# First loads of an attention and token-MLP kernel: weight quarters from two DMA queues put on one, in another order and split

## The chip, the cores and the metric

The kernel runs on one core of a Trainium2 chip. The metric is the device time of one execution in microseconds. The median of three runs before the change is 168.17 us (168.17, 168.17 and 168.28). All times below count from the start of the profiled span, in us.

## What is computed

The input is a sequence of 2048 rows of 512 (S = 2048, D = 512), all in bfloat16. Two mixers see the same rows and are blended by a gate per row:

```
qkv = x @ wqkv                       # 32 heads of 16
logits[s, w] = q[s] . k[s - 2w] / 4  # w = 0..7, only rows that exist
a = softmax(logits) @ v[s - 2w] @ wo

h = layernorm(x)                     # over the 512 columns
u = gelu(h^T @ w1 + b1)              # token MLP, 2048 -> 1792
b = (u @ w2 + b2)^T                  # 1792 -> 2048

g = sigmoid(sum(x * gate_w))
out = g * a + (1 - g) * b
```

x is A_x throughout; the layer norm, the projections and the gate all read it.

## The kernel before

**The work and its stages.** One program of about 2150 instructions. TensorE runs, in this order: a warm-up, the q and k projections of the first 512 rows, the other q and k projections, the v projections (all L619), the row sums of the q times k products (L698, in two bursts of 64), the first MLP product (L812), the second (L862) and the output projection (L878). VectorE computes the layer norm statistics (L574), the products of q and shifted k (L690), the gate sums (L674), parts of the softmax, the products with v and their sums (L797, L800, L802) and the last combination (L899). ScalarE copies results out of PSUM (L627 for q, L630 for k and v, L728 for logits, L833 gelu, L930) and normalizes rows (L598). GpSimd builds an identity matrix and zeroes paddings.

**The order.** Every operation is added to a list scheduler (`_Sched`) with a duration, the buffers it reads and writes (`reads`, `writes`), operations that it waits for (`deps`) and operations that it only follows on the same engine (`after`, `order`). The scheduler orders each engine's instructions by planned times, and semaphore waits are worked out from `deps`. A DMA given a `lands` has that planned landing time; it is used for the order alone. `chain` (L943) fixes the order on VectorE, on ScalarE and on parts of the DMA queue by hand. `last_main` chains the large matmuls in the order in which they are written.

**The first loads.** The transposed rows XT have four column blocks of 128 (block 0 to 3). For the first 512 rows:

- `d_xp` (L479, SyncE) loads the plain columns 0 to 127 of the 512 rows, 128 KB. TensorE transposes them with the identity (`f_tr`, L545, four matmuls in two operations); ScalarE copies one half (L555) and VectorE the other (L557) into column block 0 of XT.
- `d_xt0` (L473, SyncE) is a transposing DMA of the columns 128 to 511, which fills blocks 1 to 3.
- Wq, Wk and Wv are column thirds of `wqkv`; a "quarter" is the 128 rows of one that belong to one column block. `ld_w(tn, d0, n)` (L447) loads n quarters of third tn from block d0 on. The first two quarters of Wq are issued by ScalarE, two more by SyncE, then Wk in two loads of two quarters.
- After them SyncE issues `d_x0` (rows 0 to 255 for the layer norm), `d_xt1` (the transposing DMA of the next 512 rows, `ld_xt`, L460), `d_x2`, `d_x4`, `d_xt2`, `d_xt3`, `d_x8`, `d_x12`, Wv, W1 and the rest.

`throttle()` makes most later loads wait for the landing of the fifth-last one in the list `init_dmas`; `first_loads` have their waits cleared (L489).

**The first projections.** Eight PSUM banks hold q (banks 0 to 3) and k (4 to 7) of the first 512 rows, each a sum over four column blocks. L635 writes the order: q with block 0, q with 1, q with 2, q with 3, k with 0 and 1, k with 2 and 3. These are 32 matmuls; then follow the groups of four of `seq_proj` (L645) for other rows, in banks 0 to 3 again. Before them `f_warm` (L533) runs matmuls on constants: six of 512 columns (`warm1`), one of 256 (`warm2`), then the transposes, then one of 512 (`warm3`).

Of the kernel before, what the change touches and what calls it, by code (L numbers as in the profile page):

```python
# [13 lines left out]
D = 512  # L14
# [319 lines left out]
def bass_gated_mix__sliding_local_dilated__mixer_token_mlp__prompt_kernel(nc, A_x, A_wqkv, A_wo, B_x, B_w1, B_b1, B_w2, B_b2, gate_w, out, dbg=None):  # L334
    with contextlib.ExitStack() as es:
# [79 lines left out]
        A = sch.add  # L415
# [31 lines left out]
        def ld_w(tn, d0, n, q="sp"):  # L447
            ds = sch.dsem("wqkv%d_%d" % (tn, d0))
            op = sch.dma(q, mk_dma(WQKV[:, d0:d0 + n, tn * D:(tn + 1) * D], wqkv_v[:, d0:d0 + n, tn * D:(tn + 1) * D]),
                         n * 128 * D * 2, ds, writes=["wqkv%d_%d" % (tn, dt) for dt in range(d0, d0 + n)],  # L450
                         deps=throttle() if q == "sp" and n == 4 else [], after=prev_dma() if q == "sp" else [],
                         issue=0.65 if n == 4 else 0.45, name="d_wp%d_%d" % (tn, d0))
            if q == "sp":
                init_dmas.append(op)
            return op
# [14 lines left out]
        def ld_xt0():  # L470
            ds = sch.dsem("xt0")
            dst = XT[:, 1:4, 0:512]
            op = sch.dma("sp", lambda e: e.dma_start_transpose(dst, x2d[0:512, 128:512]), 512 * 384 * 2, ds, issue=1.25,  # L473
                         writes=XT0[1:4], after=prev_dma(), name="d_xt0")
            init_dmas.append(op)
            return op

        XP = view("OUTS", BF16, [(128, 4), (1, 128)])
        d_xp = sch.dma("sp", mk_dma(XP, xv[:, 0:4, 0:128]), 512 * 128 * 2, sch.dsem("xp"), writes=["outs0"], issue=0.4, name="d_xp")  # L479
        d_xp.lands = 3.9  # L480
        init_dmas.append(d_xp)

        first_loads = [ld_w(0, 0, 1, "act"), ld_xt0(), ld_w(0, 1, 1, "act"), ld_w(0, 2, 1), ld_w(0, 3, 1), ld_w(1, 0, 2), ld_w(1, 2, 2),
                       ld_x(0, 2)]
        ld_xt(1)
        first_loads.append(init_dmas[-1])
        for op_, t_ in zip(first_loads, (3.5, 5.7, 5.0, 6.3, 6.7, 7.6, 8.6, 9.4, 11.0)):
            op_.lands = t_
            op_.deps.clear()  # L489
        first_loads[2].order.add(first_loads[0])  # L490
        init_dmas[:] = [first_loads[1]] + first_loads[5:]
        ld_x(2, 2)
        ld_x(4, 4)
        ld_xt(2)
# [51 lines left out]
                return ins  # L546
            return fn

        A("pe", f_warm(6), 2.56, writes=["lg7_0", "lg7_1"], name="warm1", prio=-100)
        w2_ = A("pe", f_warm(1, 256), 0.2, writes=["lg7_0", "lg7_1"], name="warm2", prio=-100)  # L550
        ta_ = A("pe", f_tr(0), 0.215, reads=["outs0", "ident"], writes=["lg5_0", "lg5_1"], after=[w2_], name="tr0", prio=-100)
        tr_ = A("pe", f_tr(1), 0.215, reads=["outs0", "ident"], writes=["lg6_0", "lg6_1"], after=[ta_], name="tr1", prio=-100)
        A("pe", f_warm(1), 0.43, writes=["lg7_0", "lg7_1"], after=[tr_], name="warm3", prio=-100)
        w3_ = tr_
        A("act", lambda e: e.activation(out=XT[:, 0, 0:256], in_=ps[:, 5, 0:256], func=AF.Copy), 0.35, reads=["lg5_0", "lg5_1"],  # L555
          writes=["xt0_0"], name="ev_tra", prio=0)
        A("dve", lambda e: e.tensor_copy(out=XT[:, 0, 256:512], in_=ps[:, 6, 0:256]), 0.35, reads=["lg6_0", "lg6_1"],  # L557
# [74 lines left out]
        tnames = ["q", "k", "v"]  # L632
        first = [(tn, dl) for tn in range(2) for dl in range(4)]
        fbn = [["acc%d" % b] for b in range(4)] + [["lg%d_0" % b, "lg%d_1" % b] for b in range(4, 8)]
        for (b0, d0, d1, s0, s1) in ((0, 0, 1, 0, 512), (0, 1, 2, 0, 512), (0, 2, 3, 0, 512), (0, 3, 4, 0, 512), (4, 0, 2, 0, 512), (4, 2, 4, 0, 512)):  # L635
            for b in range(b0, b0 + 4):
                tn, dl = first[b]
                last_main[0] = A("pe", f_proj(tn, dl, 0, b, d0, d1, s0, s1), 0.216 * (d1 - d0) * (s1 - s0) / 512,
                                 reads=xt_of(0, d0, d1) + ["wqkv%d_%d" % (tn, dt) for dt in range(d0, d1)],
                                 writes=fbn[b], after=[last_main[0]], name="pf_%s%d_%d_%d" % (tnames[tn], dl, d0, s0))  # L640
                last_main[0].order.add(w3_)
# [411 lines left out]
```

## Time and profile before

| what | value |
|---|---|
| median of three runs | 168.17 us |
| the profiled execution's own time | 168.55 us |
| its span, first to last instruction | 167.3 us |
| TensorE busy | 163.9 us, 98% |
| VectorE busy | 151.3 us, 90% |
| ScalarE busy | 75.0 us, 45% |
| DMA moved | 29.64 MB, mean 177 GB/s |
| d_xp, issue to landing | 0.80, 3.1 us |
| first Wq quarters on ScalarE, issue to landing | 0.80 and after 1.02 us both issued, 2.9 and 3.0 us |
| d_xt0, issue, length of its issue, to landing | 1.29, 1.64, 4.4 us |
| d_xt1, the same | 5.58, 3.25, 5.5 us |
| first projection matmul | 5.15 |

In timelines each row has the start, the time that it covers, the engine ("SPq" and "ACTq" are the DMA issues of SyncE and ScalarE, "PEld" TensorE's weight loads), the line, the operation, output and input, a count, and in brackets the idle time ahead of it with what ended it. All SBUF tiles are views of one arena, so the line tells more than the name. A matmul's recorded length includes time in which the next one already runs; the distance between starts is its pace. In a table of stretches, each row gives the busy time of each engine in that stretch, then the clock, the share of the DMA engines and what they moved.

### The profile page before, as it was taken

Reading aid. Unit: us, or ns where it says so; the run is one execution under the profiler, and the core shown is the slowest. Engines: PE = TensorE matmul, PEld = TensorE weight load, DVE = VectorE, ACT = ScalarE, POOL = GpSimd, SP = SyncE. Lnnn points to the kernel's source line nnn. Section 1 sums busy time; section 2 is a strip of 40 time slices with the busy share of each in tenths; the row PEclk is TensorE's granted clock in tenths of the full one; section 3 lists DMA queues with packets and bytes.
Section 4 is the critical chain, followed back from the end, with each engine's and each line's share of the span. In section 5 each row is a group of like instructions: output and inputs, shape, how many; then the busy total and the mean of one; then the engine's idle time right before and its main releaser. Section 6 shows DMA issues by size and latency. Waiting matters only on the chain.

```text
span 167.3 us, 2152 instructions
## 1 busy us (share of the span) xinstructions
PE 163.9 (98%) x860; PEld 77.6 (46%) x860; DVE 151.3 (90%) x154; ACT 75.0 (45%) x116; POOL 0.7 (0%) x8
## 2 busy tenths in 40 slices
PE   7999999999999999999999999999999999999994
PEld 2455555554454444444444444444444444444463
DVE  0145999999999999999999999999999999999896
ACT  3077688889899818793113121131231321310100
POOL 1000000000000000000000000000000000000000
DMA  5999999968003837996579936462672580000454
GB/s 130 315 272 262 303 322 291 307 196 246 0 0 97 311 115 187 303 290 153 133 183 343 335 129 143 112 187 68 184 218 83 138 223 0 0 0 0 157 190 159
DMA packets 47625, 29.64 MB, mean 177 GB/s; under 512 B 9856, under 2 KB 46464, under 8 KB 47616
## 3 DMA queue, kind: packets, MB, share of 16 engines
q1 hardware_dynamic: 45504, 24.85, 54.0%
q10 hardware_dynamic: 2112, 4.66, 10.0%
q8 instruction: 7, 0.11, 0.3%
q14 instruction: 2, 0.02, 0.0%
HBM read 21.24 MB, written 2.10 MB: 140 GB/s over the span
## 4 chain that ended last, share of the span: by engine, by line
PE 94%; DVE 3%; DMA 2%; issue 0%
PE ps L812 29%; PE ps L862 29%; PE ps L619 25%; PE ps L878 6%; PE ps L698 4%; DVE arena L899 2%; DMA arena<-in_A_x_dram 2%; PE ps L545 0%; DVE arena L557 0%
## 5 line engine op out<-in xcount | busy, mean ns | idle before, releaser
L812 PE MATMUL ps<-arena 128*128 128x512 bf16 x224 | 48.7, 379 | 0.0
L862 PE MATMUL ps<-arena 128*128 128x512 bf16 x224 | 48.7, 379 | 0.0
L619 PE MATMUL ps<-arena 128*128 128x512 bf16 x192 | 42.3, 382 | 0.1
L690 DVE TENSOR_TENSOR arena<-arena 128x4096 bf16<-128x4096 bf16 (+1 forms) x12 | 35.5, 2996 | 2.3 <-ACT arena L630 1.8
L797 DVE TENSOR_TENSOR arena<-arena 128x8192 bf16<-128x8192 bf16 x8 | 35.0, 4419 | 0.0
L812 PEld LDWEIGHTS ps<-arena 128*128 128x128 bf16 x224 | 21.8, 98 | 26.7 <-ACT arena L728 0.4
L862 PEld LDWEIGHTS ps<-arena 128*128 128x128 bf16 x224 | 21.9, 98 | 26.5
L619 PEld LDWEIGHTS ps<-arena 128*128 128x128 bf16 x192 | 21.6, 114 | 20.8 <-DVE arena L557 0.7
L930 ACT ACTIVATE arena<-ps,arena 128x512 bf16<-128x512 f32 x16 | 12.4, 778 | 39.4 <-PE ps L862 39.4
L800 DVE TENSOR_TENSOR arena<-arena 128x4096 bf16<-128x4096 bf16 (+1 forms) x16 | 27.0, 1752 | 0.0
L630 ACT ACTIVATE arena<-ps 128x512 bf16<-128x512 f32 x32 | 18.5, 596 | 4.5 <-PE ps L619 4.5
L833 ACT ACTIVATE arena<-ps,arena 128x512 bf16<-128x512 f32 x14 | 9.6, 687 | 22.2 <-PE ps L812 17.4
L574 DVE BATCH_NORM_STATS2 arena<-arena 128x6 f32<-128x512 bf16 x16 | 10.0, 680 | 5.6 <-DMA arena<-in_A_x_dram 5.6
L878 PE MATMUL ps<-arena 128*128 128x512 bf16 (+1 forms) x80 | 14.2, 337 | 0.0
L899 DVE SCALAR_TENSOR_TENSOR arena<-ps,arena 128x512 bf16<-128x512 f32 (+1 forms) x20 | 11.5, 638 | 0.9 <-PE ps L878 0.7
L598 ACT ACTIVATE arena<-arena 128x512 bf16<-128x512 bf16 x16 | 12.2, 806 | 0.0
L627 ACT ACTIVATE arena<-ps 128x512 bf16<-128x512 f32 x16 | 9.0, 596 | 5.5 <-PE ps L619 5.4
L878 PEld LDWEIGHTS ps<-arena 128*128 128x128 bf16 x80 | 7.8, 98 | 6.3
L674 DVE SCALAR_TENSOR_TENSOR arena<-arena 128x512 bf16<-128x512 bf16 x16 | 10.1, 685 | 0.0
L744 DVE TENSOR_TENSOR arena<-arena 128x512 bf16<-128x512 bf16 (+4 forms) x11 | 7.3, 667 | 0.6 <-ACT arena L763 0.2
L698 PE MATMUL ps<-arena 128*32 128x512 bf16 x128 | 7.3, 380 | 0.0
L728 ACT ACTIVATE arena<-ps 128x512 bf16<-128x512 f32 x8 | 4.7, 592 | 4.6 <-PE ps L698 4.6
(42 smaller groups left out, 40.5 us busy)
## 6 DMA issues: line engine op xcount, KB each, us to landing
arena<-in_B_w_dram SPq DMA_DIRECT2D x7, 1024.0 KB, 8.3
arena<-in_B_w_dram SPq DMA_DIRECT2D x8, 896.0 KB, 5.1
arena<-arena ACTq DMA_DIRECT2D x32, 128.0 KB, 3.0
arena<-in_A_x_dram SPq DMA_DIRECT2D x4, 512.0 KB, 5.1
out_dram<-arena SPq DMA_DIRECT2D x14, 128.0 KB, 1.7
arena<-in_A_x_dram SPq DMA_DIRECT2D x1, 1536.0 KB, 7.9
arena<-in_A_wqkv_dram SPq DMA_DIRECT2D x2, 256.0 KB, 3.6
arena<-in_A_x_dram SPq DMA_DIRECT2D x2, 256.0 KB, 3.5
```

Of the source, the lines that this page charges most:

```text
L598: A("act", (lambda t_: (lambda e: e.activation(out=X[:, t_, :], in_=X[:, t_, :], func=AF.Identity, scale=col(RSTD, t_), bias=col(NMR, t_)) ...
L619: ins = e.matmul(ps[:, bank, s0:s1], lhsT=lhsT, rhs=XT[:, dt, sb * 512 + s0:sb * 512 + s1], start=(dt == 0 and s0 == 0), stop=(dt == 3))
L630: return lambda e: e.activation(out=dst, in_=ps[:, bank, :], func=AF.Copy)
L690: return lambda e: e.tensor_tensor(out=PBL[buf][:, :, 512 * c0:512 * (c0 + nc_)], in0=in0, in1=in1, op=ALU.mult)
L698: ins = e.matmul(ps[32 * c:32 * c + 32, 4 + wl, :], lhsT=RP, rhs=PBL[buf][:, wl, c * 512:(c + 1) * 512], start=(dl == 0), stop=(dl == 3), ...
L797: A("dve", (lambda o_, i0, i1: (lambda e: e.tensor_tensor(out=o_, in0=i0, in1=i1, op=ALU.mult)))(pv, in0, in1), 4.4, reads=v_res + ["atx_% ...
L800: A("dve", (lambda pv_, n__: (lambda e: e.tensor_tensor(out=pv_[:, 0:n__], in0=pv_[:, 0:n__], in1=pv_[:, n__:2 * n__], op=ALU.add)))(pv, n ...
L812: ins = e.matmul(ps[:, bank, :], lhsT=W1W[:, slot, st, 128 * e_:128 * e_ + 128], rhs=X[:, st, :], start=(st == 0), stop=(st == NST - 1))
L862: ins = e.matmul(ps[:, bank, :], lhsT=W2S[slot][:, ft, 128 * e_:128 * e_ + 128], rhs=UT[:, ft, :], start=(ft == 0), stop=(ft == NFT - 1))
L878: ins = e.matmul(ps[:, bank, 0:c1 - c0], lhsT=OT[:, t, 128 * i:128 * i + 128], rhs=WO[:, t, c0:c1], start=(t == 0), stop=(t == 3))
L899: A("dve", (lambda i_, b_, c0_, c1_: (lambda e: e.scalar_tensor_tensor(out=T1[:, i_, c0_:c1_], in0=ps[:, b_, 0:c1_ - c0_], scalar=col(G, i ...
L930: A("act", (lambda i_, bank_: (lambda e: e.activation(out=T1[:, i_, :], in_=ps[:, bank_, :], func=AF.Identity, scale=col(OMG, i_), bias=co ...
```

## The change

d_xp is issued first, as before. Behind it, on SyncE alone, stand now: the first quarter of Wq, the first of Wk, d_xt0, the second quarter of Wq, the second of Wk, then quarter 3 of both in one DMA and quarter 4 of both in one DMA (`ld_qk`, 256 KB each), d_xt1, d_x0. ScalarE issues none of them. d_xt1 waits until d_xt0 has landed. The first 32 projections take the order q and k with block 0, q and k with block 1, q with 2, q with 3, k with 2 and 3. The warm-up has five instead of six matmuls of 512 columns, one of 256 is added after `warm3`, and the projections follow it. The planned landing times are changed with it.

```diff
         d_xp = sch.dma("sp", mk_dma(XP, xv[:, 0:4, 0:128]), 512 * 128 * 2, sch.dsem("xp"), writes=["outs0"], issue=0.4, name="d_xp")
-        d_xp.lands = 3.9
-        init_dmas.append(d_xp)
-
-        first_loads = [ld_w(0, 0, 1, "act"), ld_xt0(), ld_w(0, 1, 1, "act"), ld_w(0, 2, 1), ld_w(0, 3, 1), ld_w(1, 0, 2), ld_w(1, 2, 2),
-                       ld_x(0, 2)]
+
+        def ld_qk(d):
+            ds = sch.dsem("wqk%d" % d)
+            op = sch.dma("sp", mk_dma(WQKV[:, d, 0:2 * D], wqkv_v[:, d, 0:2 * D]), 2 * 128 * D * 2, ds,
+                         writes=["wqkv0_%d" % d, "wqkv1_%d" % d], after=prev_dma(), issue=0.45, name="d_wqk%d" % d)
+            init_dmas.append(op)
+            return op
+
+        first_loads = [ld_w(0, 0, 1), ld_w(1, 0, 1), ld_xt0(), ld_w(0, 1, 1), ld_w(1, 1, 1), ld_qk(2), ld_qk(3)]
         ld_xt(1)
         first_loads.append(init_dmas[-1])
-        for op_, t_ in zip(first_loads, (3.5, 5.7, 5.0, 6.3, 6.7, 7.6, 8.6, 9.4, 11.0)):
+        first_loads.append(ld_x(0, 2))
+        for op_, t_ in zip(first_loads, (4.0, 4.4, 6.1, 6.5, 6.9, 7.6, 8.3, 11.3, 12.0)):
             op_.lands = t_
             op_.deps.clear()
-        first_loads[2].order.add(first_loads[0])
-        init_dmas[:] = [first_loads[1]] + first_loads[5:]
+        d_xp.lands = 3.1
+        first_loads[7].deps.add(first_loads[2])
+        first_loads[0].order.add(d_xp)
+        init_dmas[:] = [first_loads[2]] + first_loads[5:]
...
-        A("pe", f_warm(6), 2.56, writes=["lg7_0", "lg7_1"], name="warm1", prio=-100)
+        A("pe", f_warm(5), 2.13, writes=["lg7_0", "lg7_1"], name="warm1", prio=-100)
...
         A("pe", f_warm(1), 0.43, writes=["lg7_0", "lg7_1"], after=[tr_], name="warm3", prio=-100)
-        w3_ = tr_
+        w3_ = A("pe", f_warm(1, 256), 0.2, writes=["lg7_0", "lg7_1"], after=[tr_], name="warm4", prio=-100)
...
-        for (b0, d0, d1, s0, s1) in ((0, 0, 1, 0, 512), (0, 1, 2, 0, 512), (0, 2, 3, 0, 512), (0, 3, 4, 0, 512), (4, 0, 2, 0, 512), (4, 2, 4, 0, 512)):
-            for b in range(b0, b0 + 4):
+        for (b0, nb, d0, d1, s0, s1) in ((0, 8, 0, 1, 0, 512), (0, 8, 1, 2, 0, 512), (0, 4, 2, 3, 0, 512), (0, 4, 3, 4, 0, 512),
+                                         (4, 4, 2, 4, 0, 512)):
+            for b in range(b0, b0 + nb):
```

## Prediction

> **What bounds the kernel now.** I read the chain of work that ended last first, in order of time, because it tells which engine an earlier arrival would have to help.
>
> ```profile
> 0.80 3.10 DMA arena<-in_A_x_dram
> ...
> 4.04 0.60 PE ps L545 x4
> ...
> 4.66 0.44 DVE arena L557
> ...
> 5.15 33.44 PE ps L619 x152
> ...
> 161.68 3.98 DVE arena L899 x9
> ```
>
> The first transfer (d_xp) lands at 3.90, TensorE transposes it (L545), VectorE copies it out (L557), and from 5.15 to 161.68 every piece of the chain is TensorE (94% of the span by the page). So whatever lets the first projection matmuls (L619) be further along, and starves nothing later, takes the same time off the end. Those matmuls do not all run at one pace. Next, the timeline of the start (start, length, engine, count), and narrow windows of it for single starts:
>
> ```profile
> 0.84 2.93 PE L537 MATMUL ps<-const-bfloat16-1.0 128*128 128x512 bf16 x7 [0.84 <-PEq L1038]
> ...
> 5.14 0.15 PEld L619 LDWEIGHTS ps<-arena 128*128 128x128 bf16 x2 [0.68 <-DVE arena L557]
> ...
> 5.56 0.15 PEld L619 LDWEIGHTS ps<-arena 128*128 128x128 bf16 x1 [0.27 <-issue]
> ...
> 5.98 10.97 PEld L619 LDWEIGHTS ps<-arena 128*128 128x128 bf16 x51 [0.28 <-issue]
> ```
>
> The matmuls start at 5.15, 5.56, 5.98, 6.26 and 6.48, then every 0.216 us. The warm-up matmuls (L537; weight loads at 1.22, 1.64, 2.07, 2.50, 2.92) came every 0.42 to 0.43, so TensorE runs at half pace until a switch. The one that starts at 5.98 takes 0.28: u/0.427 + (0.28-u)/0.216 = 1 gives u = 0.13, so the switch is at 6.11. It is 5.27 us after the first warm-up matmul (0.84). The stretch table shows a clock of 1.00 throughout, so the pace is all that shows it. **A start that is earlier by x before 6.11 gains only half of x**, if the switch stays.
>
> Last, SyncE's queue, read with the times to landing of single DMA issues:
>
> ```profile
> 1.29 1.64 SPq L473 DMA_TRANSPOSE arena<-in_A_x_dram  x1
> 2.99 2.03 SPq L429 DMA_DIRECT2D arena<-in_A_wqkv_dram  x4
> 5.07 0.47 SPq L429 DMA_DIRECT2D arena<-in_A_x_dram  x1
> 5.58 3.25 SPq L460 DMA_TRANSPOSE arena<-in_A_x_dram  x1
> 8.87 1.09 SPq L429 DMA_DIRECT2D arena<-in_A_x_dram  x2
> ```
>
> With its time to landing, each ends at: d_xt0 1.29+4.4 = 5.7; the two quarters of Wq 2.99+3.1 = 6.1 and 3.59+2.9 = 6.5; Wk 4.08+3.4 = 7.5 and 4.55+3.8 = 8.35; d_x0 9.07; d_xt1 5.58+5.5 = 11.1. With matmul number 3 (counted from 0) at 6.26 and 0.216 each after it, TensorE needs them at number 4 (6.48), 8 (7.34), 12 (8.2), 16 (9.1) and 24 (10.8), and d_xt1 at number 32 (12.5). All are early by 0.8 us or more; only d_xp binds.
>
> **d_xp lands earlier.** Two Wq quarters (128 KB each) leave ScalarE's queue, where they were issued at 0.80 and about 1.3 beside d_xp (128 KB), and stand behind it on SyncE. The stretches about it (busy time by engine, then clock, DMA share and GB/s):
>
> ```profile
> 1.90:2.10 0.20, 0.20 (x2) 0.03 (x1) 0.00 (x0) 0.20 (x1) 0.00 (x0) 1.00 0.25 61
> 2.10:2.30 0.20, 0.20 (x2) 0.12 (x1) 0.00 (x0) 0.20 (x1) 0.00 (x0) 1.00 0.33 84
> 2.30:2.50 0.20, 0.20 (x2) 0.00 (x1) 0.00 (x0) 0.20 (x1) 0.00 (x0) 1.00 0.64 100
> 2.50:2.70 0.20, 0.20 (x2) 0.14 (x1) 0.00 (x0) 0.20 (x1) 0.00 (x0) 1.00 0.67 166
> 2.70:2.90 0.20, 0.20 (x1) 0.00 (x0) 0.00 (x0) 0.20 (x1) 0.00 (x0) 1.00 1.06 339
> ```
>
> The DMA engines are not full until 2.7. The first four sum to 82 KB, about half of it d_xp's. Alone it has some 87 KB left; at the 330 GB/s after 2.7 that is 0.26 us, to 2.96. Transfers here land 0.45 to 0.8 us after the share falls (d_x0 falls about 8.6, lands 9.07; d_xt1 10.3 and 11.1): 3.4 to 3.75. If it had had all the early bytes, 128 KB are reached at 2.85 and it lands from 3.3. The ends are the nearest rows: a 128 KB store takes 1.7 us (lands 2.5), its own row 3.1 (lands 3.9). I take 3.25, nearer the byte count than the store; the planner's due time of 3.1 is only declared.
>
> The Trainium skill, DMA: Bandwidth & Descriptors, section "Issuing engines are not separate DMA queues", says that DMAs of all issuing engines share the same 16 engines and interleave, and that several issuers save only issue time. By it the shift costs issue time and gains only what no longer interleaves with d_xp; the shares under 1 before 2.7 mean that little of that may be there, and then the first rival below holds.
>
> **From landing to the first matmul.** Landing to L545 took 4.04-3.90 = 0.14, L545 to the first projection 1.11 (4.04 to 5.15). One 512-column warm-up less ends that burst at 3.77-0.42 = 3.35, which is before 3.25+0.14 = 3.39, so it does not delay. After the transposes (4 of about 0.11) come 0.43 and the added 256-column one (0.21): 1.07, just inside the copy's 1.11; their cost is 0, and 0.2 if the copy were quicker. The first projection starts at 4.50, earlier by 0.65. By 6.11 it has done 4.50, 4.92, 5.34, 5.77 at half pace; the fourth has 0.34/0.427 = 0.80 behind it and ends at 6.15, where the kernel before reaches that point at 6.48. **Gain 0.33.** At the bounds of the landing: 2.5 is cut off by the warm-up burst (start about 4.46, gain 0.35); 3.9 gives 0.
>
> **Are later operands in time?** New queue, plain issues at 0.51 each including the gap: d_xp 0.80, Wq quarter 1.29, Wk quarter 1.80, d_xt0 2.33 to 3.97, Wq and Wk second quarters 4.03 and 4.6, d_wqk2 5.1, d_wqk3 5.6 to 6.07, then the wait. The bytes are the same 1 MB of Wq and Wk, the count of issues the same 10 (SyncE 8 to 10, ScalarE 2 to 0). A transposing transfer landed 2.2 to 2.8 us after its issue ended (2.93 to 5.7; 8.83 to 11.1): d_xt0 6.15, or 6.73 by its whole 4.4. After it the bytes went at 0.4 us per 128 KB: 6.5, 6.9, 7.7, 8.5; or, by old latencies of 3.0 to 4.0 from issue, 7.1, 7.6, 8.9, 9.6. The needs, 0.33 earlier for each number and in the new order (q and k of block 0, q and k of block 1, then q of 2, q of 3, k of 2 and 3; numbers 8, 12, 16, 20): 7.01, 7.87 for Wk's second quarter, 8.74, 9.60. I take the early ends, since the same bytes move and only the first half us at the start has fewer in flight: cost 0; the late ends cost 0.1 to 0.16. First quarters land by 1.29+3.1 = 4.4 and 4.9, need 4.50 and 6.15.
>
> **The added wait.** SyncE stands at the wait from 6.07 to d_xt0's landing (6.15; 6.73 at worst) and behind it are d_xt1, d_x0, d_x2, d_x4, the two later transposing transfers and all of W1. The 3.25 of d_xt1's issue ends when the bytes ahead have drained (d_x0's at about 8.5); the one with a free line ahead took 2.03 and the 384-column one 1.64, or 2.19 for 512. Now only Wk's 0.5 MB is ahead and d_x0 is behind: 6.2+2.2 = 8.4 to 9.4, landing 10.6 to 11.7; need 12.2. Cost 0; if d_xt0 lands at 6.73 and the old 5.5 counts from there, 12.3, and 0.1 is lost. d_xt3, before 17.8, needs 19.9: a shift of 1 us is covered.
>
> **VectorE.** d_x0 now lands at 11.3 to 12.5 and d_x2 to 13.1; four statistics (1.29 a pair) end by 13.9 to 14.7. The first product (L690) started at 15.08 on ScalarE's copy of block 1; ScalarE now copies q later (bank 0 is done at 9.96, eight copies at 0.49 to 13.95, then block 1), so this copy ends at 15.05 again: VectorE starts as before. Two later rows have the room:
>
> ```profile
> 42.20 4.43 DVE L690 TENSOR_TENSOR arena<-arena 128x8192 bf16<-128x8192 bf16 x1 [0.41 <-PE ps L698]
> 157.36 8.29 DVE L899 SCALAR_TENSOR_TENSOR arena<-ps,arena 128x512 bf16<-128x512 f32 x15 [0.72 <-PE ps L878]
> ```
>
> It waits for TensorE there, 0.41 and 0.72, so it can follow a TensorE earlier by up to 1.1. Cost 0; a VectorE late by over 0.8 would begin to eat the gain.
>
> **Sum.** -0.33 from the start, 0 for the rest. The profiled execution took 168.55 with a span of 167.3 (1.25 around it); it becomes 168.22. It lies 0.38 over the median of 168.17, so the runs should give 167.84: I say **167.85**.
>
> **Rivals.** (1) *Nothing moves.* d_xp is bound by something other than company (shares under 1 in its first 0.8 us) and lands at 3.7 to 3.9, or operands come at their late ends (7.1 for 7.01, 12.3 for 12.2) and take 0.2 back: 168.05 to 168.2. (2) *The switch moves with the work.* If full pace comes after so much busy time, before it had 2.93+0.86+0.96 = 4.75 us by 6.11 with 0.5 us of holes; the new order has 2.51 by 3.35 and almost no hole, and reaches 4.75 at 5.65. By then 2.7 matmuls are done, by 6.11 4.8 against 2.3: gain 0.54; with a switch earlier still, up to 0.84, where the second Wq quarter at 6.5 binds (number 8 was at 7.34): 167.3 to 167.65. For it: the switch fell 5.27 after the first matmul though 4.75 were busy. Against: nothing here shows two switches to compare. (3) *The switch is lost.* One warm-up less leaves TensorE idle from 3.35 to d_xp's landing + 0.14. Before, that hole was 0.27 (3.77 to 4.04). If a longer hole restarts the count, from a landing past 3.48 the switch comes 5.27 after the transposes, at about 8.9 instead of 6.11, and half of 2.8, less the gain of 0.2, is lost: 169.4; a partial restart, 168.5 to 169.4. Against: 0.27 was survived, and the added matmul closes the 0.25 before 5.15.
>
> The Trainium skill, TensorE: Matmul & The Clock Gate, Part 1, has windows of about 3.4 us that run free of the kernel and release the clock after a busy one. By it the switch sits at a boundary whatever the extra work does, as in my sum, which would be 0.33 by it and 0.54 by counted work. Its phase would differ from run to run; the three runs, within 0.11 us, do not show that.
>
> **Chances.** Forecast 0.40 (gain 0.1 to 0.4), rival 1 0.15, rival 2 0.25, rival 3 0.20, with any case of operands so late that they cost over 0.4. About 0.2% (0.34 us) is what a measurement can tell from no change. The forecast splits at it, 0.16 above and 0.24 below: faster 0.16+0.25 = 0.41, same 0.24+0.15 = 0.39, slower 0.20. The range leaves out most of rival 3 and the far end of rival 2: 167.35 to 168.6; the forecast's own is 167.75 to 168.1.
>
> **What would show it.** d_xp landing at 3.1 to 3.4 and L545 0.14 later; the first L619 near 4.5; weight loads 0.42 apart up to the switch, and where it falls (6.1: forecast; 5.7 or less: rival 2; 8 or later: rival 3); no hole in L619 near 7.0, 8.7, 9.6 and 12.2; d_xt1 landed by 11.7; the VectorE wait of 0.41 at 42 shorter or gone. A landing of d_xp as late as 3.9 or a hole over 0.3 in L619 would make it wrong.

## The result and the profile after

The changed kernel takes **168.65 us** in the median of 21 runs (168.20 to 169.42); beside it the kernel before took 168.18 us in 21 runs (167.84 to 168.91). The ratio, worked out from all the runs and so not exactly that of the two medians, is 1.0025, with a 95% interval of 1.0014 to 1.0036: **slower, by 0.47 us between the medians**. 167.85 had been predicted.

The profiled execution of the changed kernel took 168.50 us, with a span of 167.2. Before, these were 168.55 and 167.3. So the two profiled executions are level although the medians are 0.47 us apart. That is the first thing to explain: one of the two is not typical of its kernel. The execution of 168.55 is slower than 17 of the 21 times of the kernel before; that of 168.50 is below the median of its own.

The changed lines move the numbers: L545 becomes L552, L537 L544, L557 L564, L619 L626, L690 L698 and L899 L907. The chain of work that ended last, in order of time (start, length, what):

```profile
3.34 0.55 PE ps L552 x4
...
4.53 2.74 PE ps L626 x8
7.31 6.42 PE ps L626 x29
...
161.65 3.98 DVE arena L907 x9
```

The transposes start at 3.34 instead of 4.04: the first transfer (d_xp) did land earlier. But the last VectorE chain starts at 161.65 instead of 161.68. The break between the eighth projection and the ninth, at 7.31, shows where to look. TensorE's weight loads of the changed kernel:

```profile
4.41 0.14 PEld L626 LDWEIGHTS ps<-arena 128*128 128x128 bf16 x2 [0.57 <-DVE arena L564]
...
6.10 0.15 PEld L626 LDWEIGHTS ps<-arena 128*128 128x128 bf16 x1 [0.28 <-issue]
6.46 0.33 PEld L626 LDWEIGHTS ps<-arena 128*128 128x128 bf16 x2 [0.21 <-issue]
7.28 1.45 PEld L626 LDWEIGHTS ps<-arena 128*128 128x128 bf16 x8 [0.49 <-issue]
```

The projections begin at 4.41, 0.74 us earlier than before (5.15). They run at half pace, one every 0.42, up to a switch at about 6.39 (the step from 6.10 to 6.46 is 0.36, so 0.29 of it is at half pace). After it number 5 starts at 6.46, and number 8 could start at 6.46 + 3 x 0.216 = 7.11. It starts at 7.31, and number 16 at 9.04. Before, number 8 started at 7.34 and number 16 at 9.07. So 0.74 us of earlier start has become 0.03 within eight matmuls: half pace and a switch 0.28 us later take 0.51, and a wait of 0.20 for the second quarter of Wq takes the rest.

SyncE's queue of the changed kernel (start, length of the issues, line, operation, count):

```profile
0.80 0.45 SPq L429 DMA_DIRECT2D arena<-in_A_x_dram  x1
1.31 0.96 SPq L429 DMA_DIRECT2D arena<-in_A_wqkv_dram  x2
2.32 1.86 SPq L473 DMA_TRANSPOSE arena<-in_A_x_dram  x1
4.23 2.00 SPq L429 DMA_DIRECT2D arena<-in_A_wqkv_dram  x4
6.71 2.81 SPq L460 DMA_TRANSPOSE arena<-in_A_x_dram  x1
```

and times to landing, as the list of DMA issues in the first 20 us has them (KB each, median us):

```profile
arena<-in_A_wqkv_dram SPq DMA_DIRECT2D x4, 128.0 KB, 2.9
arena<-in_A_wqkv_dram SPq DMA_DIRECT2D x2, 256.0 KB, 3.7
arena<-in_A_x_dram SPq DMA_DIRECT2D x1, 128.0 KB, 2.4
```

d_xp lands at 0.80 + 2.4 = 3.2. The issue of d_xt0 begins a microsecond later than before (2.32 against 1.29) and lasts 1.86, and in that time SyncE sends nothing else. d_xt0 lands at 6.7. The four loads behind it, each with its own latency, land at 4.23 + 2.95 = 7.2 (Wq's second quarter), 4.86 + 2.8 = 7.7 (Wk's), 5.32 + 3.6 = 8.9 (d_wqk2) and 5.80 + 3.8 = 9.6 (d_wqk3). The wait before d_xt1 is 6.23 to 6.71.

What that queue does to the DMA engines is in the table of stretches (busy time by engine, then clock, DMA share, GB/s). The kernel before:

```profile
3.00:3.90 0.90, 0.77 (x3) 0.07 (x1) 0.00 (x0) 0.13 (x1) 0.00 (x0) 1.00 1.18 317
3.90:4.80 0.90, 0.76 (x5) 0.45 (x5) 0.14 (x1) 0.35 (x1) 0.00 (x0) 1.00 1.28 278
```

and the changed kernel:

```profile
3.00:3.90 0.90, 0.90 (x7) 0.56 (x6) 0.00 (x0) 0.19 (x1) 0.00 (x0) 1.00 0.58 188
3.90:4.80 0.90, 0.90 (x3) 0.14 (x2) 0.42 (x1) 0.20 (x1) 0.00 (x0) 1.00 0.85 115
```

From 1.8 to 4.8 the kernel before moves 722 KB and the changed one 509; by 8.4 it is 1871 against 1469. A second execution of each (b1 and a1 below) has 712 against 516 by 4.8 and 1720 against 1486 by 8.4. The bytes to be moved are the same. They are sent later.

VectorE did not hold TensorE back. At 42.18 its wait for TensorE ahead of the second product (L698) is 0.38 (before 0.41).

### The profile page after: what moved, and what is told of

Same layout as the page of the kernel before. It is cut to its first block, busy times and chain, and to the rows that moved or that the text cites. A ratio compares the mean times of both kernels' runs of the same rounds, so it can differ in the third digit from the quotient of the medians.

```text
span 167.2 us, 2138 instructions
## 1 busy us (share of the span) xinstructions
PE 163.3 (98%) x846; PEld 77.7 (46%) x860; DVE 151.1 (90%) x154; ACT 74.8 (45%) x116; POOL 0.7 (0%) x8
## 3 DMA queue, kind: packets, MB, share of 16 engines
q10 hardware_dynamic: 1824, 4.39, 9.4%
## 4 chain that ended last, share of the span: by engine, by line
PE 96%; DVE 2%; issue 1%
PE ps L870 29%; PE ps L820 29%; PE ps L626 25%; PE ps L886 6%; PE ps L706 4%; DVE arena L907 2%; PE ps L544 2%; PE ps L552 0%
## 5 line engine op out<-in xcount | busy, mean ns | idle before, releaser
L626 PE MATMUL ps<-arena 128*128 128x512 bf16 x188 | 42.5, 385 | 0.4 <-ACT arena L594 0.2
L698 DVE TENSOR_TENSOR arena<-arena 128x4096 bf16<-128x4096 bf16 (+1 forms) x12 | 35.4, 2994 | 0.4 <-PE ps L706 0.4
L626 PEld LDWEIGHTS ps<-arena 128*128 128x128 bf16 x192 | 21.6, 114 | 21.4 <-issue 1.8
L938 ACT ACTIVATE arena<-ps,arena 128x512 bf16<-128x512 f32 x16 | 12.5, 778 | 39.4 <-PE ps L870 39.4
L637 ACT ACTIVATE arena<-ps 128x512 bf16<-128x512 f32 x32 | 18.7, 599 | 3.2 <-PE ps L626 3.1
L634 ACT ACTIVATE arena<-ps 128x512 bf16<-128x512 f32 x16 | 9.3, 603 | 8.1 <-PE ps L626 8.1
L907 DVE SCALAR_TENSOR_TENSOR arena<-ps,arena 128x512 bf16<-128x512 f32 (+1 forms) x20 | 11.5, 638 | 0.9 <-PE ps L886 0.7
L736 ACT ACTIVATE arena<-ps 128x512 bf16<-128x512 f32 x8 | 4.7, 592 | 4.6 <-PE ps L706 4.6
```

The lines of the kernel that those rows point to most:

```text
L626: ins = e.matmul(ps[:, bank, s0:s1], lhsT=lhsT, rhs=XT[:, dt, sb * 512 + s0:sb * 512 + s1], start=(dt == 0 and s0 == 0), stop=(dt == 3))
L637: return lambda e: e.activation(out=dst, in_=ps[:, bank, :], func=AF.Copy)
L698: return lambda e: e.tensor_tensor(out=PBL[buf][:, :, 512 * c0:512 * (c0 + nc_)], in0=in0, in1=in1, op=ALU.mult)
L907: A("dve", (lambda i_, b_, c0_, c1_: (lambda e: e.scalar_tensor_tensor(out=T1[:, i_, c0_:c1_], in0=ps[:, b_, 0:c1_ - c0_], scalar=col(G, i ...
L938: A("act", (lambda i_, bank_: (lambda e: e.activation(out=T1[:, i_, :], in_=ps[:, bank_, :], func=AF.Identity, scale=col(OMG, i_), bias=co ...
```

## The experiments

Each kernel was run beside the kernel before on the same chip; the ratios are to that kernel, with a 95% interval. The theories, by the letters that some expectations use: the single line of SyncE brings the later operands late (A, later L); the switch of pace moves or is lost (S); the shorter warm-up costs (C); the added wait costs (W); the last transposing DMA, d_xt3, comes too late (D).

**e1: the second quarters on ScalarE.** The changed kernel, with both second quarters on ScalarE's queue, in program order behind an added one-element activation that was to keep them clear of d_xp.

```diff
-first_loads = [ld_w(0, 0, 1), ld_w(1, 0, 1), ld_xt0(), ld_w(0, 1, 1), ld_w(1, 1, 1), ld_qk(2), ld_qk(3)]
+first_loads = [ld_w(0, 0, 1), ld_w(1, 0, 1), ld_xt0(), ld_w(0, 1, 1, "act"), ld_w(1, 1, 1, "act"), ld_qk(2), ld_qk(3)]
+tab_ = A("act", lambda e: e.activation(out=col(TH, 0), in_=nc.const_aps.tensor(1.0, [128, 1], BF16), func=AF.Copy), ...
+first_loads[3].order.add(tab_)
+first_loads[4].order.add(first_loads[3])
```

> The changed kernel, but the second quarters of Wq and Wk are issued by ScalarE, behind a one-element copy that has the activation table loaded first (so from about 2.3 us, and not beside d_xp). Theory A (one line runs dry: while SyncE spends 1.86 us issuing d_xt0, nothing else is issued, the DMA engines move 110 to 220 GB/s from 3.0 to 4.8 where they moved 250 to 350, and the operands of matmuls 8 and 16 land at 7.1 and 8.9, which gives the early start back): both quarters land by 6.0, the wait at matmul 8 shrinks to what d_xt0 (6.7) sets, the one at matmul 16 goes because d_wqk2 is issued 1 us earlier; 0.2 to 0.5 us under the changed kernel's 168.65: 168.15 to 168.45. Theory W (the added wait costs it, by d_xt1 and all behind it): d_xt0 lands no earlier, the wait ends no earlier, so 168.5 to 168.8. Theory C (the shorter warm-up makes full pace come later): no change, 168.5 to 168.8.

169.23 (168.05 to 170.61, 12 runs), ratio 1.0058 [1.0026, 1.0089]. The edit did not do what it was meant to. ScalarE in its trace:

```profile
0.86 0.97 ACTq L429 DMA_DIRECT2D arena<-in_A_wqkv_dram  x2
2.09 0.20 ACT L478 ACTIVATE arena<-const-bfloat16-1.0 128x1 f32<-128x1 bf16 x1
```

The loads went out at 0.86, beside d_xp, though they stand behind the activation that ran at 2.09. d_xp landed at 3.9, as before the change, and the start was 5.18. That shows what held d_xp in the kernel before: two loads in its company cost it 0.7 us. The spread of 2.4 us, even without the slowest run, is new; the profiled execution (168.10) is at its lower end and does not show its cause.

**e2: the wait away.**

```diff
-        first_loads[7].deps.add(first_loads[2])
```

> The changed kernel without the wait of d_xt1 for d_xt0. A: d_xt1 is issued at about 6.25 instead of 6.71 and lands earlier, but TensorE did not wait for it, so the same time, 168.5 to 168.8. W: back to 168.2 or under. C: 168.5 to 168.8.

168.79 (168.22 to 169.83, 12), 1.0034 [1.0013, 1.0056]. The loss stays, so the added wait is not its cause.

**e3: the sixth warm-up matmul back.**

```diff
-        A("pe", f_warm(5), 2.13, writes=["lg7_0", "lg7_1"], name="warm1", prio=-100)
+        A("pe", f_warm(6), 2.56, writes=["lg7_0", "lg7_1"], name="warm1", prio=-100)
```

> The changed kernel with six instead of five long warm-up matmuls, so the first projection starts about 0.4 us later, at 4.8. A: the operands of matmuls 8 and 16 are what it waits for (7.1, 8.9), so the later start costs only part of 0.4: 168.65 to 168.85, and the wait at matmul 8 is gone or smaller. C: full pace comes earlier again and 168.2 or under results. If the early start were worth half of itself, as the prediction had it, 168.85 to 168.9.

169.20 (168.52 to 169.72, 11), 1.0044 [1.0023, 1.0064]. The shorter warm-up is not the cause either. Its switch came early, at 5.1, and the ninth matmul then waited 0.36 for the weights. The matmuls of its trace also show a second floor that I had not priced:

```profile
7.17 13.12 PE L626 MATMUL ps<-arena 128*128 128x512 bf16 x59 [0.36 <-DMA arena<-in_A_wqkv_dram]
21.26 9.01 PE L626 MATMUL ps<-arena 128*128 128x512 bf16 x40 [0.96 <-DMA arena<-in_A_x_dram]
```

Number 68 is the first that needs d_xt3, and it stood 0.96 us, until d_xt3 had landed at 21.1.

**e4 and e5: a start that is the same in every execution.** To take the switch out of the comparison, I held back the first projections of the kernel before until d_xt1 (e4) or d_x0 (e5) had landed, and filled the time with warm-up matmuls.

```diff
-        A("pe", f_warm(1), 0.43, writes=["lg7_0", "lg7_1"], after=[tr_], name="warm3", prio=-100)
-        w3_ = tr_
+        w3_ = A("pe", f_warm(21), 5.0, writes=["lg7_0", "lg7_1"], after=[tr_], name="warm3", prio=-100)
-                                 reads=xt_of(0, d0, d1) + ["wqkv%d_%d" % (tn, dt) for dt in range(d0, d1)],
+                                 reads=xt_of(0, d0, d1) + xt_of(1) + ["wqkv%d_%d" % (tn, dt) for dt in range(d0, d1)],
```

e5 has `f_warm(14)` there, and `deps=[first_loads[7]]` on the first projections in place of `xt_of(1)`.

> The kernel before, with 21 long warm-up matmuls behind the transposes and the first projection held until d_xt1 has landed (11.1), so that every execution starts its projections at full pace and at a landing. About 168.18 + 5.6 to 6.0 = 173.8 to 174.2. If the spread of the kernel's runs (167.84 to 168.91 in 21) comes from a switch of pace that falls at another time in each execution, the 5 or more runs of this one lie within 0.4 us; if it comes from elsewhere, they spread over 0.7 us or more.

> The kernel before, with 14 instead of one long warm-up matmuls behind the transposes and the first projection held until d_x0 has landed (9.1 to 9.7), so TensorE idles under 2 us and starts its projections after the switch of pace in every execution. Theory S (the switch falls at another time in each execution; in the traces so far at 6.1, 6.4, under 5.2, under 4.7, about 5.1 and 4.3; half of what lies between 5.15 and it is lost): 172.0 to 172.8 with a spread under 0.7 us, where the kernel before spreads over 1.1 to 1.4. If the spread of the kernel before comes from its transfers or later stages: the same 1.1 to 1.4 or more here.

e4: 176.29 (175.26 to 178.11, 6); e5: 173.69 (172.49 to 174.39, 4). Both failed as a test: the runs spread over 1.3 us (e4, without its slowest) and 1.9 us (e5), where under 0.4 and 0.7 had been expected. The warm-up was too short and TensorE idled ahead of the first projection (3.35 us by its matmuls in e4, 2.15 in e5). e5's weight loads, and the stretches of its trace, show what can follow:

```profile
9.64 0.80 PEld L618 LDWEIGHTS ps<-arena 128*128 128x128 bf16 x5 [2.62 <-issue]
...
13.95 0.98 PEld L618 LDWEIGHTS ps<-arena 128*128 128x128 bf16 x5 [0.21 <-issue]
```

```profile
10.46:13.87 3.41, 3.41 (x10) 1.18 (x8) 1.56 (x3) 0.00 (x0) 0.00 (x0) 0.50 1.05 287
```

After the idle time five loads come at full pace, then one every 0.43 until 13.95: the pace was lost again for 3.41 us, and in just this stretch the granted clock is 0.50. So half pace here is half the granted clock. e4's profiled execution idled longer, 3.35 us, and all its projections run at full pace; the length of the idle time alone does not decide.

**e6: three loads on ScalarE, held until VectorE's first reduction.** Wk's first quarter and both second quarters on ScalarE, the first of them after VectorE's small reduction of the identity matrix (`rp_`).

```diff
-first_loads = [ld_w(0, 0, 1), ld_w(1, 0, 1), ld_xt0(), ld_w(0, 1, 1), ld_w(1, 1, 1), ld_qk(2), ld_qk(3)]
+first_loads = [ld_w(0, 0, 1), ld_w(1, 0, 1, "act"), ld_xt0(), ld_w(0, 1, 1, "act"), ld_w(1, 1, 1, "act"), ld_qk(2), ld_qk(3)]
+first_loads[1].deps.add(rp_)
+first_loads[3].order.add(first_loads[1])
+first_loads[4].order.add(first_loads[3])
```

> The changed kernel, but Wk's first quarter and the second quarters of Wq and Wk are issued by ScalarE, held until VectorE's first reduction (about 1.5 us), so that they are generated while SyncE issues d_xt0, and not at 0.8 beside d_xp. Theory A (SyncE alone runs dry while it issues d_xt0): d_xp lands by 3.4, d_xt0 by 6.3, the second quarters by 6.2, d_wqk2 by 7.6; no wait at matmuls 8 and 16; 167.4 to 167.9 with the ratio to the kernel before under 0.999. Rival B (the DMA engines were full anyway and only share out the same bytes): d_xp lands at 3.6 or later, d_xt0 at 6.6 or later, and 168.2 to 168.7 results.

169.77 (169.06 to 170.0, 6), 1.0073 [1.005, 1.0096]. Neither theory had these numbers. d_xp landed at 3.2, but the start was 4.75, since ScalarE loaded its activation table only behind the three issues (2.92 to 4.20) and copied its half of block 0 at 4.22. d_xt0, issued at 1.85, took 5.7 us to land (7.55) beside the three plain loads of the other queue. So a second queue is no cure by itself: it matters what its loads run beside.

**e7: e1 with six warm-up matmuls.** The edit to e1:

```diff
-        A("pe", f_warm(5), 2.13, ...
+        A("pe", f_warm(6), 2.56, ...
```

> The kernel of e1 (second quarters on ScalarE, in fact issued at 0.86 beside d_xp, which then landed at 3.9) with six instead of five long warm-up matmuls. In e1's trace TensorE idled from 3.35 to 4.03. Theory H (a hole of 0.7 us there lets the switch come later in many executions): median from 169.23 to 168.0 to 168.5 and spread from 2.5 us to under 1.5. If e1's spread comes from its transfers: 169.0 to 169.4 and a spread of 2 or more.

168.77 (168.13 to 169.32, 12), 1.0012 [0.9987, 1.0037]; the spread falls to 1.19. In e1's trace the idle time ahead of the transposes is long (0.69), and one more matmul fills 0.42 of it. That a hole there sometimes costs the switch would explain the times of 170 us and more in e1, but none of those was profiled, so this is suggested and not shown.

**b1: the kernel before, profiled once more.** No edit.

> The kernel before once more, for its switch of pace. Theory S: its time is 167.85 plus half of what lies between 5.15 and the switch (0 if the switch comes before 5.15), within 0.2 us. If the time does not follow the switch, S falls.

168.03 us, span 166.7. This run explains the first puzzle. Its projections:

```profile
4.98 25.23 PE L619 MATMUL ps<-arena 128*128 128x512 bf16 x116 [0.30 <-DVE arena L557]
```

They start at 4.98 and are at full pace from the first on: already the 512-column warm-up matmul behind the transposes took 0.38 and not 0.63. This trace also has a record of the granted clock, which stands at full from 3.55 on; so the switch was there. Number 8 starts at 6.73 and number 16 at 8.46, 0.61 earlier than in the profiled execution of before. **The switch of pace falls at another time in each execution**, and the kernel before can use an early one. It only just can: number 4 starts at 5.87 for a d_xt0 that landed at 5.7, number 16 at 8.46 for a load that landed at 8.3.

**e8 and e9: d_x4 behind the last transposing loads,** in the changed kernel (e8) and in the one before (e9), to bring d_xt3 earlier.

```diff
-        ld_x(4, 4)
         ld_xt(2)
         ld_xt(3)
+        ld_x(4, 4)
```

> The changed kernel with d_x4 (512 KB for VectorE's statistics) moved behind d_xt2 and d_xt3. Theory D (besides the waits at matmuls 8 and 16, the change pushes d_xt3 from 17.8 to 18.4 in the kernel before to 19.8 to 21.2 in the traces of the changed one and its variants, because d_x0, d_x2 and d_x4 now all drain ahead of d_xt2; TensorE needs d_xt3 at its matmul 68, at about 20.3, and stalled 0.96 us for it in the six-warm-up variant): d_xt3 lands by 18.7, the slow executions go, median 168.15 to 168.45, spread under 0.9 us. Theory A alone (only the waits at 8 and 16): no change, 168.5 to 168.8 as the changed kernel in the same call.

> The same move of d_x4 behind d_xt3 in the kernel before. D: d_xt3 is over 1 us early there, so nothing is gained: within 0.1 us of the kernel before; VectorE's later statistics might cost up to 0.2. If the move itself were worth something, 0.2 us or more faster.

e8: 168.86 (168.46 to 169.24, 12), 1.0027 [1.0012, 1.0041]; e9: 168.66 (167.84 to 169.22, 12), 1.0014 [0.9996, 1.0032]. In e8 d_xt3 lands at 18.2 and there is no hole at number 68, but beside the changed kernel itself on the same chip (a1, below) that gains only 0.1 us, which the two intervals do not tell from nothing. Its first matmuls say why:

```profile
7.31 23.04 PE L626 MATMUL ps<-arena 128*128 128x512 bf16 x104 [0.90 <-DMA arena<-in_A_wqkv_dram]
```

The start was 4.39 and the switch came at 4.7, so eight matmuls were done by 6.4. The ninth then stood 0.90 for the weights and started at 7.31, and number 16 at 9.04, both as in the first profile of the changed kernel, whose switch came 1.7 us later. The same move seems to cost the kernel before a little; its interval holds 1, and whether the late d_x4 is the reason is open: in its trace the switch is early (3.84), but number 16 stands 0.2 for a weight load that landed at 8.7 and that is ahead of the moved one in the queue.

**e10: d_x0 ahead of d_xt1 again,** so that the layer norm's rows stand where they stood before.

```diff
+        first_loads.append(ld_x(0, 2))
         ld_xt(1)
         first_loads.append(init_dmas[-1])
-        first_loads.append(ld_x(0, 2))
```

> The changed kernel with d_x0 ahead of d_xt1 again, and so ahead of the wait, as in the kernel before. D with the order of d_x0 as its cause: d_xt2's issue (4.3 to 5.4 us in the variants, 3.5 before) shortens and d_xt3 lands by 19.2: 168.2 to 168.5. If the lateness comes from the start of the line (0.7 us of bytes missing by 4.8, the wait, 1 us of issues more), d_xt3 lands at 19.5 or later and 168.5 to 168.8 results.

169.01 (168.55 to 169.35, 8), 1.0038 [1.0021, 1.0055]. The order of d_x0 is not the cause. The ninth matmul again stands, for 0.59. Number 68 starts at 20.74, 0.05 behind the pace.

**a1: the changed kernel, profiled once more.** No edit.

> The changed kernel again, beside the three others on the same chip. A and D: matmul 16 not before 9.0 whatever the switch does, and if this execution takes over 168.8, a hole of TensorE at matmul 68 for d_xt3. Median 168.5 to 168.8.

168.97 (168.35 to 169.39, 12), 1.0036 [1.002, 1.0052]; the profiled execution took 169.28, span 168.0. Its matmuls:

```profile
4.39 2.37 PE L626 MATMUL ps<-arena 128*128 128x512 bf16 x8
7.34 13.12 PE L626 MATMUL ps<-arena 128*128 128x512 bf16 x59 [0.58 <-DMA arena<-in_A_wqkv_dram]
21.02 9.23 PE L626 MATMUL ps<-arena 128*128 128x512 bf16 x41 [0.56 <-DMA arena<-in_A_x_dram]
```

This is the other half of the puzzle. The switch came at 5.4, one us earlier than in the first profile, and eight matmuls were done by 6.76. The ninth waited 0.58 for a quarter of the weights and started at 7.34, where it had started with the late switch. **The changed kernel cannot use an early switch**, because its operands come no earlier (7.2 in both traces).

**e11: everything of the change but the one line.** The order of the loads and of the projections, the split and the wait are kept; the two first quarters (of Wq and of Wk) go to ScalarE's queue, with the six warm-up matmuls.

```diff
-first_loads = [ld_w(0, 0, 1), ld_w(1, 0, 1), ld_xt0(), ...
+first_loads = [ld_w(0, 0, 1, "act"), ld_w(1, 0, 1, "act"), ld_xt0(), ...
...
-        first_loads[0].order.add(d_xp)
+        first_loads[1].order.add(first_loads[0])
+        first_loads[2].order.add(d_xp)
...
-        A("pe", f_warm(5), 2.13, ...
+        A("pe", f_warm(6), 2.56, ...
```

> The changed kernel, but ScalarE issues the first quarters of Wq and Wk at 0.80, so that two loads leave SyncE as in the kernel before; six long warm-up matmuls. Order, split and wait of the change stay. Theory L (the loss is that of one line: two issues more ahead of and behind d_xt0, with nothing else issued while its 1.6 to 1.9 us pass): the start falls back to about 5.0, d_xt0 lands at 5.7, d_wqk2 by 7.6, d_xt3 by 18.7, and the time is that of the kernel before within 0.2 us: 168.15 to 168.55. Theory O (the new order asks for both first and second quarters too early, or the wait costs): waits at matmuls 8 and 16 remain, 168.6 to 169.1.

168.14 (167.91 to 168.97, 12), 0.999 [0.9972, 1.0008]: the loss is gone. From e3 (1.0044) this kernel differs in the queue of these two loads alone. SyncE and TensorE in its trace:

```profile
1.31 2.27 SPq L473 DMA_TRANSPOSE arena<-in_A_x_dram  x1
3.63 1.99 SPq L429 DMA_DIRECT2D arena<-in_A_wqkv_dram  x4
```

```profile
4.88 25.44 PE L627 MATMUL ps<-arena 128*128 128x512 bf16 x115 [0.19 <-DVE arena L565]
```

d_xp lands at 3.8 again and the start is 4.88. But d_xt0 is issued at 1.31 and lands at 5.7, 1.0 earlier than in the changed kernel, the four loads behind it leave at 3.63 instead of 4.23, and with a switch at 3.54 TensorE runs without a hole: number 16 starts at 8.36. By 8.4, 1676 KB have been moved, against 1469.

**e12: the one line alone.** The kernel before, its two ScalarE loads put on SyncE, with the warm-up of the change.

```diff
-first_loads = [ld_w(0, 0, 1, "act"), ld_xt0(), ld_w(0, 1, 1, "act"), ld_w(0, 2, 1), ...
+first_loads = [ld_w(0, 0, 1), ld_xt0(), ld_w(0, 1, 1), ld_w(0, 2, 1), ...
...
-        first_loads[2].order.add(first_loads[0])
...
-        A("pe", f_warm(6), 2.56, ...
+        A("pe", f_warm(5), 2.13, ...
-        w3_ = tr_
+        w3_ = A("pe", f_warm(1, 256), 0.2, writes=["lg7_0", "lg7_1"], after=[tr_], name="warm4", prio=-100)
```

> The kernel before with its two ScalarE loads (first and second quarter of Wq) on SyncE, one ahead of and one behind d_xt0, and the warm-up of the change; order of the projections, split of Wk and d_xt1 as before. L: d_xp lands at 3.2 and the start is 4.4 to 4.5, but matmul 4 waits for the second quarter (issued at about 3.6, landing at 6.5 to 6.7), number 16 comes at 9.2 or later, d_xt3 lands at 19 or later: 168.5 to 169.2. O: the early start is kept in part and 167.9 to 168.3 results.

169.53 (169.15 to 171.29, 9), 1.0076 [1.0048, 1.0103]: slower by 1 us. Its matmuls:

```profile
4.28 1.39 PE L618 MATMUL ps<-arena 128*128 128x512 bf16 x4
7.01 6.21 PE L618 MATMUL ps<-arena 128*128 128x512 bf16 x28 [1.34 <-DMA arena<-in_A_wqkv_dram]
13.75 16.57 PE L618 MATMUL ps<-arena 128*128 128x512 bf16 x74 [0.54 <-DMA arena<-in_A_x_dram]
```

It has the earliest start of all, 4.28. (The warm-up came with it; e3 and e14 show that the warm-up alone does not make such a loss.) In the old order TensorE needs Wq's second quarter as early as number 4, and that lands at 3.54 + 3.3 = 6.84. The new order of the projections, with k's first quarter ahead, is what keeps this hole small in the changed kernel; it mends what the one line breaks, and not all of it.

**e14: the holes of the kernel before filled.** `warm2` is 512 wide instead of 256, and the added warm-up matmul of 256 is taken over.

```diff
-            w2_ = A("pe", f_warm(1, 256), 0.2, ...
+            w2_ = A("pe", f_warm(1, 512), 0.4, ...
-        w3_ = tr_
+        w3_ = A("pe", f_warm(1, 256), 0.2, writes=["lg7_0", "lg7_1"], after=[tr_], name="warm4", prio=-100)
```

> The kernel before with 256 columns more of warm-up ahead of the transposes and one more matmul of 256 behind them, which fills the idle 0.27 and 0.25 us of TensorE there. Theory S/H (the switch of pace comes sooner the fewer holes the start has, and half of what lies between 5.15 and it is lost): 168.0 to 168.3, 0.1 to 0.3 us under the kernel before. If holes this small do not matter: within 0.1 us of it.

168.68 (168.09 to 169.02, 12), 1.0003 [0.9985, 1.002]. Filling holes of 0.27 and 0.25 does nothing that the time shows; in its profiled execution (169.02) the switch came at 6.8, later than in any other trace. So there is no sign that more work in the warm-up brings the switch earlier.

**e15 and e11b: e11 with the old tail (d_x0 ahead of d_xt1, no wait), and e11 again.** The edit of e15 to e11:

```diff
+        first_loads.append(ld_x(0, 2))
         ld_xt(1)
         first_loads.append(init_dmas[-1])
-        first_loads.append(ld_x(0, 2))
...
-        first_loads[7].deps.add(first_loads[2])
```

The planned landing times are changed with it.

> The kernel of e11 (first quarters on ScalarE, new order and split of the projections) with d_x0 ahead of d_xt1 and no wait, as in the kernel before, so that of the change only the order and split of the weight loads and the 256 columns of warm-up are left. L: operands and d_xt3 (by 18.6) are as early as in the kernel before, 168.0 to 168.5 with the interval around 1. O: slower than 1.002. If the e11 time (168.14) came from d_xt1 going out ahead of d_x0, this one is 0.2 us or more slower than e11.

> The kernel of e11 again on the same chip as e15, since its interval (0.9972 to 1.0008) does not settle whether it beats the kernel before: if it does, the ratio is under 0.999 again; if d_xt3 (19.3 in its trace, needed at 19.6) comes late in many executions, over 1.

e15: 168.24 (168.01 to 168.9, 11), 1.0002 [0.9986, 1.0017]; e11b: 168.44 (167.99 to 169.09, 12), 1.0008 [0.9991, 1.0025]. Both are level with the kernel before. Without the one line, the rest of the change costs nothing and brings nothing that these runs can tell (all three intervals hold 1; that of e11b still allows a loss of up to 0.25%); no version beat the kernel before.

**The traces together.** Every execution below without a later hole ends 158.2 to 158.3 us after number 16 has started, so this one start tells the time. Where a trace has a record of the granted clock, the switch is the time from which the clock is full (b1, e11, e9, a1, e2, e3, e8, e12); in the others it is worked out from the distances of the starts. Where both can be had they agree within 0.1 us. A later hole is idle time of TensorE behind number 16. Left out are e4 and e5, whose starts were held back, and e1, e6 and e7, which put other loads on ScalarE.

| execution | time, us | start | switch | number 16 | later hole | span |
|---|---|---|---|---|---|---|
| before | 168.55 | 5.15 | 6.11 | 9.07 | - | 167.3 |
| before (b1) | 168.03 | 4.98 | 3.55 | 8.46 | - | 166.7 |
| e9 | 168.33 | 4.96 | 3.84 | 8.78 | - | 167.1 |
| e14 | 169.02 | 5.22 | 6.8 | 9.45 | - | 167.7 |
| e11 | 167.91 | 4.88 | 3.54 | 8.36 | - | 166.6 |
| e15 | 168.76 | 5.24 | 6.45 | 9.29 | - | 167.5 |
| e11b | 168.91 | 5.12 | 6.7 | 9.35 | - | 167.6 |
| after | 168.50 | 4.41 | 6.4 | 9.04 | - | 167.2 |
| after (a1) | 169.28 | 4.39 | 5.4 | 9.07 | 0.56 | 168.0 |
| e2 | 168.58 | 4.44 | 4.4 | 9.01 | - | 167.3 |
| e3 | 169.50 | 4.72 | 5.1 | 8.90 | 0.96 | 168.2 |
| e8 | 168.60 | 4.39 | 4.7 | 9.04 | - | 167.3 |
| e10 | 168.98 | 4.44 | 6.1 | 9.47 | - | 167.7 |
| e12 | 169.77 | 4.28 | 5.0 | 9.60 | 0.54 | 168.5 |

The seven rows with two loads on ScalarE follow the switch: an early one gives 8.4 to 8.8, a late one 9.1 to 9.45. The seven with one line do not: with switches from 4.4 to 6.4, number 16 starts at 8.9 or later, and in three of them something is late again behind it.

## Why the prediction was wrong, step by step

**What bounds the kernel:** right. In the traces without a later hole the end follows TensorE's progress at number 16 to a tenth, and VectorE's waits stayed (0.38 and 0.74 us, before 0.41 and 0.72).

**d_xp lands earlier:** right, 3.2 for 3.25. e1 and e11, where two loads run beside it again, have 3.8 to 3.9.

**From landing to the first matmul:** right, 4.41 for 4.50; nothing in the warm-up delayed it.

**The gain of 0.33:** right in form, wrong in what it took as fixed. With the switch at 6.11 the start of 4.41 would give half of 0.74, 0.37. The reading that TensorE runs at half pace up to a switch holds in every trace. But I took the switch of one execution for that of the kernel. It lies anywhere between 3.5 (e11) and 6.8 (e14). With a switch before the start the earlier start would even count in full, some 0.57 (4.41 against b1's 4.98), if the operands were there. The Trainium skill, TensorE: Matmul & The Clock Gate, Part 1, has a window that runs free of the kernel, so that the phase varies from run to run; the prediction set this aside because three times lay within 0.11 us. The 21 times of the same kernel spread over 1.07 us, and b1 beside before shows the switch in it: on the variation the traces agree. They also fit such a window: in e5 the clock changes at 3.64, 10.46 and 13.87, twice and once 3.41 us apart, and the first switches of all traces lie within 3.3 us.

**"Are later operands in time?" is the step that failed.** It worked out two sets of landings and took the early one: 6.5, 6.9, 7.7 and 8.5. They came at 7.2, 7.7, 8.9 and 9.6, the late set almost to the tenth (7.1, 7.6, 8.9, 9.6), and d_xt0 at 6.7, its late value too (6.73). The reason given, that the bytes are the same and only the first half microsecond has fewer in flight, was wrong: 213 KB are missing by 4.8 and 402 by 8.4 (196 and 234 between b1 and a1). SyncE has two issues more to make ahead of d_xt0, 1.0 us, and while it issues d_xt0 nothing else goes out, where in the kernel before ScalarE had sent its two loads by then. The 1.86 us of d_xt0's issue is not itself new: it was 1.64 and 2.10 in the two traces of the kernel before. The price put on the late set, 0.1 to 0.16, was also too small. It was worked out against needs that were only 0.33 earlier, with the switch at 6.11; with a switch before the start at 4.41, number 8 would be at 6.14 and number 16 at 7.87 (8 x 0.216 each), 0.87 earlier than those needs, and the landings stay. e8, with its switch at 4.7, shows it: number 8 at 7.31 and number 16 at 9.04. e11 against e3 (the loss goes when the two loads leave the line, and nothing else differs) and e12 (1.0076 when they join it, with the warm-up of the change) show the cause from both sides.

The price fits the medians. Of the kernel before, the median of 168.18 lies between the times of b1 (168.03, switch at 3.55) and of the first profile (168.55, switch at 6.11). The changed kernel has a floor: its fastest of 21 is 168.20, where the kernel before reaches 167.84. 12 of the 21 times before are under that floor. What an early switch gives is lost: with those of a1, e8 and e2 number 16 came no earlier than 9.0.

**"The added wait: cost 0":** right as far as e2 can tell. SyncE stood 6.23 to 6.71 and d_xt1 landed at 11.6; number 32 started at 12.5 without a wait.

**"d_xt3 ... a shift of 1 us is covered":** wrong. It landed at 19.8 in the first profile and at 20.9 and 21.1 in a1 and e3, 2.0 to 3.3 later than 17.8 (b1 had 18.4), since d_xt2's issue also grew, from 3.5 us to 4.3 and more, with d_x0, d_x2 and d_x4 queued ahead of it. In the first profile number 68 started at 20.27 and just missed the hole; in a1 TensorE idled 0.56 there. e8 shows it is a second floor, not the main one: without the hole at most 0.1 us is gained.

**The sum's offset.** I took 0.38 us between the profiled execution and the median for a constant of the measurement. It was in the main the late switch of that one execution: b1, with an early one, lies 0.15 below 168.18. In the changed kernel the offset is -0.15.

**The rivals.** The mechanism that came true is that of the first one, operands at their late ends, but it was put down as "nothing moves" with a price of 0.2. Operands so late that they cost over 0.4 were named only in a half sentence of the chances, within the 0.20 for slower, and not worked out. The second, a switch that moves with the work, is spoken against by e14. The third, a lost switch, is not in the trace of the changed kernel; it may be in those times of e1, and stays open there.

## What to carry to other kernels

An issuing engine is a resource with a length of its own: count what its queue holds and for how long each issue lets nothing else out, above all for transposing DMAs, before two queues are put on one; the transfer that this speeds up is paid for by all that stand behind it. When one wait is shortened, put the next operands' landings against the needs of the best execution, not of the one in the profile. And where the pace of an engine changes at a time that differs between executions, take a second profile before anything is read from the first: a difference of 0.5 us between two executions of one kernel was larger than the effect here.

## What the runs showed of the hardware

- Two executions of one kernel differed in the switch of TensorE's pace by 2.6 us (3.55 in b1, 6.11 before), which moved the end by 0.5 to 0.6 us; over all traces it lay between 3.5 and 6.8, with the first matmul at 0.83 or 0.84. Nine of the 19 traces, that of before among them, hold no record of the granted clock; the 1.00 in their tables of stretches stands beside matmuls 0.42 apart, so it does not tell the pace there.
- An idle time of only 2.15 us ahead of 9.67 (e5) was followed by 3.41 us at a granted clock of 0.50, some 1.7 us lost. The pace fell only 0.8 us after TensorE had begun again. One of 3.35 us ahead of 12.48 (e4) was followed by full pace.
- ScalarE's DMA issues went out at 0.86 although they stood behind an activation that ran at 2.09 (e1). Order on an engine did not hold a DMA back there.
- Two plain loads beside d_xp moved its landing from 3.2 to 3.9, and three beside d_xt0 made it take 5.7 us instead of 4.4 (e6). The Trainium skill, DMA: Bandwidth & Descriptors, section "Issuing engines are not separate DMA queues", says that transfers of all issuing engines interleave on the same DMA engines; these rows agree. It also says that a second issuer saves only issue time, usually a small thing. Here that issue time decides: two issues of half a microsecond ahead of d_xt0, whose own issue then holds the line for 1.86 us, are what the one line lost.
- The issue of a transposing DMA of 512 columns grew with the loads queued ahead of it: d_xt2's took 2.4 us with one load between it and d_xt1 (e9), 2.8 to 4.2 with two (e8, before, e10) and 4.3 to 5.4 with three (the changed kernel, a1, e3).
